# Reordering the first loads and the fillers, and holding back the second tile, at the head of a one-core FFT convolution

## The chip, the cores and the metric

The kernel runs on one core of one Trainium2 chip. The metric is the device time of an execution in microseconds (us). Within a time or a mean, a run is one execution; e1 to f4 below are experiments of several runs each. Where kernels are compared, they ran on the same chip in alternating rounds, and "ratio" is the mean time of one kernel's fast runs over the mean of the other's fast runs of the same rounds, so it is not quite the ratio of the medians that are quoted beside it. On one core a run is called slow when it is more than 1.5% above the fastest of its kernel. Lower is better, and a verdict of faster needs more than 2%.

## The reference

A 7 x 7 convolution of a 224 x 224 x 96 image, done through Fourier transforms, all in bf16 at the ends:

```python
x: (1, 224, 224, 96) bf16      w: (7, 7, 96, 96) bf16
wp = pad(w, to (224, 224))
Xf = rfft2(x over h, w);  Wf = rfft2(wp over h, w)
Yf = einsum('bhwi,hwio->bhwo', Xf, Wf)
y  = irfft2(Yf).astype(bf16)
```

## The kernel before

The kernel transforms along the image's height only, in blocks (matrix `Fm`), convolves along the width with few-tap products in that domain, and transforms back (matrix `G`). The image is cut into seven tiles of 32 columns. Each tile's pixels are loaded in two halves (`jg` 0 and 1, 118 rows each), multiplied by `Fm` on TensorE and evicted from PSUM into `xf`. The weights are loaded once as 98 rows and transformed by matmuls from `wq` into `WF`, in six groups; only the first group (48 matmuls, 12 evictions) is needed before the rounds can begin.

The head, all that comes before the first round, is what the change touches. First the loads, all issued by SyncE in this order: four small halo loads, the weights, the first tile, the second tile.

```python
for jg in range(2):
    load_rows(xh_bufs[jg], jg, W - PAD, PAD)                 # halo
dma(wqx[0:2*(PW-1), 0:C*C], bass.AP(wsrc.tensor, wsrc.offset, [[C*C, PW-1], [C2, 2], [1, C*C]]))   # 96 rows
for h in range(2):                                            # the last two rows, one by one
    n = C*C - h*C2
    dma(wqx[2*(PW-1)+h:2*PW-1+h, 0:n], wsrc[PW-1:PW, h*C2:])
for t in range(2):
    for jg in range(2):
        load_x(t, jg)                                         # 112 + 6 rows of 6,144 bytes each
...
warm(8); warm(9)                 # fillers: 128 x 512 matmuls on zeros, meant to keep TensorE's clock up
```

Then the order of work on TensorE, which follows the program:

```python
xf0 = new_xf(0)
for jg in range(2):
    for f in a_bank(0, xf0, xh_bufs[jg], 0, 3, jg, 0):        # halo: 12 matmuls
        f()
warm(8); warm(8)
fj = [f_jobs(0, p) for p in range(3)]
for f in prep_jobs(0) + fj[0][0] + fj[1][0] + fj[2][0] + fj[0][1]:
    f()                          # 48 weight matmuls, 96 on the first half of the pixels, 32 on the second
for f in jit(0, 0):              # sums on VectorE for the first rounds
    f()
...                              # rounds: products of xf and WF, each with more of the above as fill
```

## Time and profile before

How to read the lines: PE is TensorE (matmuls), PEld its weight loads, DVE is VectorE, ACT is ScalarE, POOL is GpSimd, and SP is SyncE, which issues the loads. A record is one instruction in the trace. The granted clock is the share of full speed at which TensorE is allowed to run (1.00 or 0.50 here). A frequency-domain matmul is one of `pb<-WF,xf`, the product of transformed weights and pixels; the first of them marks the end of the head.

| | before |
|---|---|
| median, and range of 4 runs | 295.09 us, 294.56 to 295.59 |
| span of the profiled run | 291.1 us (the run took 292.79 us, 2.3 us under the median) |
| TensorE idle before the weights | 6.00 us, from 10.45 to 16.44 us |
| TensorE idle at its 450th record | 2.28 us, from 24.23 to 26.51 us |
| half clock | 14.02 to 20.85 and 27.68 to 31.09 us, and the last 0.6 us |
| first frequency-domain matmul | 26.54 us |

The page's first line gives the busy time of each engine, its share of the span and the number of its instructions:

```profile
PE 268.3 (92%) x5227; PEld 242.7 (83%) x5227; DVE 223.2 (77%) x453; ACT 196.7 (68%) x485; POOL 113.8 (39%) x166
```

TensorE (PE) is the bound over the whole kernel, with 22.8 us of idle time in 291.1. Of these some 8.3 us are the two holes at the head. Busy time counts a matmul at half clock as longer (fillers follow one another every 0.23 us at full clock here, 16 in 3.62 us, and every 0.43 us at half clock in the changed kernel, from 21.09 us), so the half-clock stretches hide more of the loss inside the 268 us. How these places are found is told in the prediction.

### The profile page before, as it was taken

Reading aid. Unit: us, or ns where it says so; the run is one execution under the profiler, and the core shown is the slowest. Engines: PE = TensorE matmul, PEld = TensorE weight load, DVE = VectorE, ACT = ScalarE, POOL = GpSimd, SP = SyncE. Lnnn points to the kernel's source line nnn. Section 1 sums busy time; section 2 is a strip of 40 time slices with the busy share of each in tenths; the row PEclk is TensorE's granted clock in tenths of the full one; section 3 lists DMA queues with packets and bytes.
Section 4 is the critical chain, followed back from the end, with each engine's and each line's share of the span. In section 5 each row is a group of like instructions: output and inputs, shape, how many; then the busy total and the mean of one; then the engine's idle time right before and its main releaser. Section 6 shows DMA issues by size and latency. Waiting matters only on the chain.

```text
span 291.1 us, 12374 instructions
## 1 busy us (share of the span) xinstructions
PE 268.3 (92%) x5227; PEld 242.7 (83%) x5227; DVE 223.2 (77%) x453; ACT 196.7 (68%) x485; POOL 113.8 (39%) x166
## 2 busy tenths in 40 slices
PE   8476999899999979999999998999999999998982
PEld 4176999899999979988899987989898988886961
DVE  6146499888988869879977888787997789776823
ACT  6056997668764536886788867897788865657213
POOL 7711034248446564332643227222543324322100
PEclk9959899999999999999999999999999999999999
DMA  6993010441111289978659585787539543857846
GB/s 154 214 238 84 2 45 5 142 142 45 43 56 47 87 239 201 284 190 239 187 145 252 157 255 149 199 233 240 180 93 254 164 131 110 226 164 198 230 115 190
DMA packets 43857, 46.07 MB, mean 158 GB/s; under 512 B 33303, under 2 KB 34435, under 8 KB 43703
## 3 DMA queue, kind: packets, MB, share of 16 engines
q1 hardware_dynamic: 41512, 43.22, 53.9%
q10 hardware_dynamic: 2288, 2.06, 2.2%
q8 instruction: 41, 0.67, 1.0%
q14 instruction: 16, 0.12, 0.1%
HBM read 23.93 MB, written 21.33 MB: 155 GB/s over the span
## 4 chain that ended last, share of the span: by engine, by line
PE 59%; DVE 17%; DMA 11%; issue 4%; ACT 4%; POOL 1%; SPq 1%; DVEq 0%; ACTq 0%
PE pb L85 59%; DVE J L85 7%; DMA wq<-in_w_dram 4%; DVE WF L85 3%; DVE v L85 3%; DMA xn<-in_x_dram 2%; DVE u L85 2%; DVE yf L85 2%; DMA tt<-scr 1%; DMA out_dram<-yo 1%; DMA scrb<-yf 1%; ACT xf L85 1%; DMA xf<-scrb 1%; ACT WF L85 1%; SPq L85 1%
## 5 line engine op out<-in xcount | busy, mean ns | idle before, releaser
L85 PE MATMUL pb<-WF,J 96*128 96x96 bf16 x2898 | 169.0, 206 | 1.3 <-DVE u L85 0.8
L85 PEld LDWEIGHTS <-J 96*128 96x128 bf16 x2898 | 141.6, 98 | 17.0 <-issue 10.7
L85 POOL TENSOR_TENSOR yf<-v,u 128x384 bf16<-128x384 f32 x85 | 83.8, 1000 | 144.3 <-issue 96.4
L85 ACT CAST xf<-pb 96x408 bf16<-96x408 f32 (+3 forms) x146 | 68.6, 486 | 10.7 <-PE pb L85 8.3
L85 ACT CAST yo<-pb 84x384 bf16<-84x384 f32 (+1 forms) x144 | 61.4, 482 | 9.3 <-DMA out_dram<-yo 4.3
L85 DVE TENSOR_TENSOR J<-xf 96x1824 bf16<-96x1824 bf16 (+1 forms) x84 | 63.0, 789 | 0.1
L85 PE MATMUL pb<-WF,xf 96*128 96x96 bf16 x952 | 60.0, 206 | 0.1
L85 PEld LDWEIGHTS <-xf 96*128 96x128 bf16 x952 | 47.1, 98 | 2.6 <-issue 2.6
L85 PE MATMUL pb<-Fm,xn 118*128 118x136 bf16 (+3 forms) x640 | 46.0, 199 | 3.2 <-DMA xn<-in_x_dram 2.0
L85 PE MATMUL pb<-tt,Gm 102*84 102x384 bf16 (+1 forms) x144 | 36.3, 329 | 2.8 <-DVE u L85 1.2
L85 ACT CAST WF<-pb 96x480 bf16<-96x480 f32 (+1 forms) x63 | 31.2, 574 | 11.0 <-PE pb L85 10.9
L85 PEld LDWEIGHTS <-xn 118*128 118x128 bf16 x640 | 30.5, 97 | 3.6 <-DMA xn<-in_x_dram 2.2
L85 PE MATMUL pb<-wq 98*128 98x120 bf16 (+1 forms) x288 | 23.1, 240 | 6.0 <-DMA wq<-in_w_dram 6.0
L85 DVE TENSOR_TENSOR J<-J 96x912 bf16<-96x912 bf16 (+1 forms) x42 | 27.1, 646 | 0.0
L85 PEld LDWEIGHTS <-wq 98*128 98x128 bf16 x288 | 21.0, 151 | 6.5 <-issue 6.5
L85 POOL COPY xf<-xf 96x816 bf16<-96x816 bf16 (+3 forms) x20 | 17.3, 889 | 1.4 <-DVE xf L85 1.4
L85 DVE TENSOR_TENSOR yf<-v,u 128x384 bf16<-128x384 f32 x27 | 15.5, 575 | 0.9
L85 PE MATMUL pb<-wu 128*112 128x384 bf16 (+1 forms) x69 | 14.8, 375 | 1.1 <-DVE ct L85 1.1
L85 PEld LDWEIGHTS <-Gm 102*84 102x84 bf16 (+1 forms) x144 | 11.5, 114 | 4.0 <-issue 1.4
L85 PEld LDWEIGHTS <-wu 128*112 128x112 bf16 (+1 forms) x69 | 8.1, 119 | 6.7 <-issue 1.8
L85 DVE CAST WF<-pb 96x400 bf16<-96x400 f32 (+1 forms) x9 | 5.4, 604 | 9.4 <-PE pb L85 9.1
L85 DVE TENSOR_TENSOR WF<-WF 96x960 bf16<-96x960 bf16 x15 | 10.7, 763 | 0.6 <-ACT WF L85 0.6
(390 smaller groups left out, 219.8 us busy)
## 6 DMA issues: line engine op xcount, KB each, us to landing
scr<-yf SPq DMA_DIRECT2D x30, 288.0 KB
xn<-in_x_dram SPq DMA_DIRECT2D x12, 672.0 KB
tt<-scr SPq DMA_DIRECT2D x24, 288.0 KB
out_dram<-yo SPq DMA_DIRECT2D x24, 252.0 KB
tt<-scr SPq DMA_DIRECT2D x12, 192.0 KB
out_dram<-yo SPq DMA_DIRECT2D x12, 168.0 KB
wq<-in_w_dram SPq DMA_DIRECT2D x1, 1728.0 KB
WF<-in_x_dram SPq DMA_DIRECT2D x2, 672.0 KB
```

The source lines that it names most:

```text
L85: r = fn(*a, **k)
```

## The change

The intent: use the wait for the weights for half of the first tile's work, shorten the wait at its end, keep the second tile's 1.4 MB out of the way until the head is through, and place the fillers anew.

```diff
     for jg in range(2):
         load_rows(xh_bufs[jg], jg, W - PAD, PAD)
-    dma(wqx[0:2 * (PW - 1), 0:C * C], bass.AP(wsrc.tensor, wsrc.offset, [[C * C, PW - 1], [C2, 2], [1, C * C]]))
-    for h in range(2):
-        n = C * C - h * C2
-        dma(wqx[2 * (PW - 1) + h:2 * PW - 1 + h, 0:n], wsrc[PW - 1:PW, h * C2:])
-    for t in range(2):
-        for jg in range(2):
-            load_x(t, jg)
+    load_x(0, 0)
+    for k, n in ((0, PW - 1), (PW - 1, 1)):
+        dma(wqx[2 * k:2 * (k + n), 0:WC], bass.AP(wsrc.tensor, wsrc.offset + k * C * C, [[C * C, n], [C2, 2], [1, WC]]))
+    load_x(0, 1)
... (WC = C * C - C2; the matrix Em and the zeros behind it move to column WC; loads and evictions return their instruction)
-    warm(8)
-    warm(8)
     fj = [f_jobs(0, p) for p in range(3)]
-    for f in prep_jobs(0) + fj[0][0] + fj[1][0] + fj[2][0] + fj[0][1]:
+    for p in range(3):
+        for f in fj[p][0]:
+            f()
+    for _ in range(2):
+        warm(8)
+    for f in prep_jobs(0):
         f()
+    warm(4)
+    last = [f() for f in fj[0][1]]
+    for jg in range(2):
+        for d in load_x(1, jg):
+            tc.add_manual_dep(d.ins, last[0].ins.name, SYNC, reason="second tile's pixels later")
```

More of the change, by code (lines that the diff above doesn't have):

```diff
@@ L151 @@
     wq = wqx[0:PW2]
-    Em = wqx[0:PW2, C * C:C * C + 2 * NSLOT * NTAP].rearrange("p (h a t) -> p h a t", h=2, a=NSLOT)
+    WC = C * C - C2
+    Em = wqx[0:PW2, WC:WC + 2 * NSLOT * NTAP].rearrange("p (h a t) -> p h a t", h=2, a=NSLOT)
     XHW = PAD * C + 32
@@ L163, in ld @@
         def ld(p0, p1, hh):
-            dma(xb[p0:p1, 0:n], x[0, hh:hh + (p1 - p0), w0:w0 + npx, :].rearrange("h w c -> h (w c)"))
-        ld(PAD, R, h0 + PAD)
-        ld(0, PAD, h0 % H)
+            return dma(xb[p0:p1, 0:n], x[0, hh:hh + (p1 - p0), w0:w0 + npx, :].rearrange("h w c -> h (w c)"))
+        return ld(PAD, R, h0 + PAD), ld(0, PAD, h0 % H)
     def xbuf(t, jg):
@@ L171, in load_x @@
     def load_x(t, jg):
-        load_rows(xbuf(t, jg), jg, t * 2 * TW, 2 * TW)
+        return load_rows(xbuf(t, jg), jg, t * 2 * TW, 2 * TW)
     wsrc = w.rearrange("kh kw i o -> (kh kw) (i o)")
@@ L213 @@
     SE.activation(out=dmy[:], in_=pi_t[:], func=ACTF.Sin, bias=0.0, scale=0.0)
-    zw = wqx[0:PW2, C * C + 2 * NSLOT * NTAP:]
+    zw = wqx[0:PW2, WC + 2 * NSLOT * NTAP:]
     SE.copy(out=zw, in_=wu[0:PW2, 0:1].to_broadcast(list(zw.shape)))
@@ L432, in f @@
                 pi = pa[0:C, 0:(b - a) * n].rearrange("c (w r s j) -> c r s w j", r=2, s=s1 - s0, w=b - a)
-                apart(("A", t), (a, jg, ph, part), evac(xo, pi, (b - a) * n))
+                return apart(("A", t), (a, jg, ph, part), evac(xo, pi, (b - a) * n))
             return f
```

## The prediction

> **What bounds the kernel now.** I read the page first, then stretches cut at the steps of the granted clock, then the first 36 us of the chain of waits, the timeline there, and the records of packets and landings. The first two lines below are the page's busy digits and granted clock in 40 slices of 7.3 us.
>
> ```profile
> PE   8476999899999979999999998999999999998982
> ...
> PEclk9959899999999999999999999999999999999999
> ```
>
> From the sixth slice on TensorE is nearly full; the loss is in the first five slices, the head, and it is the only place besides the end where the clock falls. The stretches of 3.41 us show it (columns: stretch, length, busy us and count for PE, PEld, DVE, ACT and POOL, granted clock, DMA share, GB/s):
>
> ```profile
> 10.61:14.02 3.41, 0.00 (x0) 0.00 (x0) 0.00 (x0) 0.00 (x0) 2.77 (x11) 1.00 0.88 195
> 14.02:17.44 3.42, 1.00 (x13) 1.03 (x14) 0.11 (x1) 0.44 (x1) 1.81 (x5) 0.50 0.98 229
> 17.44:20.85 3.41, 3.41 (x47) 3.41 (x45) 2.69 (x5) 2.58 (x7) 0.00 (x0) 0.50 1.03 238
> 20.85:24.26 3.41, 3.38 (x123) 3.28 (x121) 3.17 (x7) 2.87 (x7) 0.00 (x0) 1.00 0.91 208
> 24.26:27.68 3.42, 1.17 (x22) 1.17 (x22) 1.09 (x3) 1.57 (x5) 1.00 (x3) 1.00 0.09 36
> 27.68:31.09 3.41, 3.41 (x51) 3.41 (x49) 2.67 (x4) 3.06 (x8) 0.30 (x1) 0.50 0.02 5
> ```
>
> Two holes stand out, at 10.45 to 16.44 us and at 24.23 to 26.51 us, and each is followed by a stretch at half clock. The timeline and the chain name what ended them:
>
> ```profile
> 16.44 3.77 PE L85 MATMUL pb<-wq 98*128 98x100 bf16 x43 [6.00 <-DMA wq<-in_w_dram]
> ...
> 26.51 0.19 PE L85 MATMUL pb<-Fm,WF 118*128 118x64 bf16 x1 [2.28 <-POOL xf L85]
> ```
> ```profile
> 3.61 12.70 DMA wq<-in_w_dram
> ```
>
> *First hole.* TensorE waits for the weights. The records of landings split the wait: the 96-row transfer is complete at 13.49 us, the first single row at 14.53, the second at 16.31. The packets of 18,432 bytes take 1.32 us in the median, and the two last rows follow one another (the last packet runs 13.11 to 14.89). So the last 2.82 us of the wait are two rows of 18 KB, queued behind each other.
>
> *Second hole.* It is put down to GpSimd's halo copy, which I don't believe: that copy ended at 26.10 and feeds the other buffer. What does fit is an instruction fetch. The trace has 41 packets of 16,384 bytes on the "instruction" queue for 10,516 TensorE records, 256 each. The first of them in the span runs from 23.80 to 25.06 us; TensorE stands still at its 450th record and goes on 1.45 us after the packet. The next packet starts at 27.91, 1.40 us after TensorE goes on. [...] The first-tile and second-tile pixels filled the DMA engines at that time (share 0.91 to 1.03), the second tile landing only at 27.12.
>
> [...] steps at 14.02, 20.85, 27.68 and 31.09 us, all multiples of 3.41 apart; a window only 1.17 us busy also led to half clock.
>
> **The change part by part.**
> 1. *First pixels ahead of the weights.* Two issues (0.3 to 0.4 us each) move in front of the weights; that alone costs nothing, because the rings are busy with the halo rows until 3.62 us. The data is what costs: 118 rows of 6,144 bytes, [...] a packet takes 0.415 us, so 8 x 0.415 = 3.3 us. Weight packets then start at about 6.9 instead of 3.88 us: +3.0 us.
> 2. *Last two rows in one transfer.* [...] So the weights should be complete at 14.53 + 3.0 = 17.5 us, against 16.31: they come 1.2 us later, where without this part it would be 3.0. All 18,336-byte rows are 0.5% shorter, which is nothing.
> 3. *Work moved into the hole.* The 96 matmuls on the first half (29 ns apart at full clock, 2.8 us) and their ten evictions (0.6 us each on two engines, 3 us) move from after the weights to about 7.5 to 10.5 us. Sixteen fillers (3.62 us before) then keep TensorE busy to about 14. Idle remains 14 to 17.5 us.
> 4. *After the weights.* 48 weight matmuls: 82 to 85 ns apart at half clock before, so 4.0 us; at full clock 62 ns (later weight matmuls), so 3.0 us. One window between 14 and 17.5 is mostly idle, so I count part of it at half clock: 3.6 us, to 21.2. Four fillers 0.9, to 22.1. Then 32 matmuls, 0.9, to 23.0. The second half of the pixels is ready: [...] weights through at 13.1 + 3.0 = 16.1, then 8 x 0.415, then up to 1 us of landing, so 20.4. The third of the last four evictions ends about 0.4 us after the last matmul: the first frequency-domain matmuls start at 23.4, against 26.54 before: **-3.1 us**.
> 5. *Instruction block.* [...] the 2.28 us stall goes. This is contained in point 4, not added to it.
> 6. *Clock after the head.* Without the second hole there should be no half-clock stretch from 27.68 to 31.09. It held 51 matmuls; at full clock that is about 1.7 us less TensorE time, but ACT was 3.06 us busy in the same stretch, and the chain goes over to ACT's weight evictions at 30.75. I count half: **-0.8 us**.
> 7. *Second tile held.* Issued near 22.3 us, landed after about 1.2 us of issue and start and 3.1 us for each half: 26.6 and 29.7. In the kernel before, the first half was used 8.3 us and the second 12.2 us after the first frequency-domain matmul, so at 31 and 35 here: hidden. Its 1.4 MB do meet the next instruction block[...]: 0 to 1 us, counted as 0.
>
> Sum: 3.1 + 0.8 = 3.9 us. From 60 to 280 us TensorE is 97% busy in an unchanged program, so a shift of the head should reach the end whole. 294.73 - 3.9 = 290.8.
>
> **The rivals.**
> *The weights' delay eats the gain.* If TensorE falls to half clock for everything from 17.5 on, fillers included (0.43 us each, as the first six fillers show), the last matmul of the head is at 17.5 + 4.0 + 1.7 + 1.8 = 25.0, a gain of 1.5 us only: 293.2. For it: idle of 3.5 us, [...]
> *The stall moves.* The held pixels occupy the engines just when the next block is fetched; [...] up to 1 us back, 291.8. For it: the delay seen before. [...]
> *Everything goes well.* If the landing's lag of 1.4 us shrinks and the clock holds, the first frequency-domain matmul is at 21.5 to 22, and the half-clock stretch is all gain: 5.5 to 6 us, 289. For it: the fillers were surely sized for it. Against: the bytes ahead of the weights can't be argued away.
> *The gain is lost in 30 to 50 us.* There ACT and DVE are on the chain, evicting weights and first products. Those jobs are unchanged and start earlier with the head; I see nothing absolute in time there except the second tile's arrival, with 4 us to spare.
>
> **Range and chances.** The two bad rivals together make about 293, the good one 289; nothing brings it over 295 unless the held pixels arrive late. 2% is 5.9 us and needs every uncertain term on the good side: 14%. Slower by 2% would need a new wait of 10 us: 2%.
>
> **What would show it.** Weights complete at 17 to 18 us and the 96 early matmuls before 11; no hole of 2 us near the 450th TensorE record; the first frequency-domain matmul between 22 and 24.5; granted clock full from about 24 us; second tile's pixels landed before they are read. It would be wrong if the weights land after 18.5 us, if TensorE stops again for an instruction block at 27 to 30 us, or if the second tile is waited for near 31 us.

## The result

The changed kernel took 291.41 us in the median (290.87 to 292.21, 4 runs) against 295.09 us (294.56 to 295.59, 4 runs): 3.7 us less. The ratio is 0.9878, with a 95% interval of 0.9846 to 0.991: by the 2% rule the same, yet clear of noise. The prediction had 290.8 us, 3.9 us under the 294.73 us that it started from. Two later measurements of the same kernel on other chips gave 0.9846 and 0.9869.

The profile after, first the page's busy line and its rows of 40 slices:

```profile
PE 271.0 (94%) x5231; PEld 243.1 (84%) x5231; DVE 223.9 (77%) x453; ACT 197.2 (68%) x485; POOL 114.9 (40%) x166
...
PE   8959998999999979999999998999999999999982
...
PEclk9988999799999999999999999999999999999998
```

The second slice of TensorE, 4 before, is 9, and the third, now with the rest of the wait for the weights, is 5 instead of 7; the clock now also dips in the eighth slice, near 51 us, where it was full before. Next the stretches between the steps of the clock (columns as in the prediction):

```profile
16.69:20.10 3.41, 2.25 (x36) 2.28 (x37) 1.77 (x4) 1.52 (x4) 0.00 (x0) 1.00 0.25 69
20.10:23.52 3.42, 3.42 (x33) 2.32 (x32) 1.42 (x3) 1.38 (x4) 0.00 (x0) 0.50 0.00 0
23.52:26.93 3.41, 2.97 (x74) 2.85 (x72) 3.03 (x5) 3.07 (x8) 1.98 (x3) 1.00 0.58 156
26.93:30.34 3.41, 3.41 (x79) 3.41 (x76) 1.28 (x2) 3.41 (x10) 0.33 (x1) 1.00 0.95 267
```

The half-clock stretch at 27.68 us is gone: 79 matmuls run in 3.41 us where 51 did. But one of 3.41 us lies within the head, from 20.10 us, and only 33 matmuls start in it. The timeline shows which (columns: start, length, engine, operation, count; in brackets the idle time before and what ended it):

```profile
8.61 2.69 PE L85 MATMUL pb<-Fm,WF 118*128 118x64 bf16 x96 [0.35 <-DMA WF<-in_x_dram]
...
11.15 3.61 PE L85 MATMUL pb<-wu 128*128 128x512 bf16 x16
...
17.85 3.44 PE L85 MATMUL pb<-wq 98*128 98x100 bf16 x48 [3.09 <-DMA wq<-in_w_dram]
...
21.09 1.91 PE L85 MATMUL pb<-wu 128*128 128x512 bf16 x4
...
22.79 1.44 PE L85 MATMUL pb<-Fm,WF 118*128 118x64 bf16 x32
...
24.66 0.52 PE L85 MATMUL pb<-WF,xf 96*128 96x96 bf16 x8 [0.44 <-ACT xf L85]
```

The 96 early matmuls fill part of the wait. The weights come at 17.72 us, the 48 weight matmuls still run mostly at full clock, and then the four late fillers take 1.91 us at half clock, before the last 32 matmuls. The first frequency-domain matmul (`WF,xf`) starts at 24.66 us, 1.9 us earlier than before. The hole of 2.28 us is gone.

Between these two profiles the spans differ by only 2.0 us (289.1 against 291.1), less than the 3.7 us between the medians. Two things make the difference. The profile of before was of a run 2.3 us under its median, that of after of a run 0.5 us under. And the clock dip near 51 us cost the changed kernel a part of its gain. The stretches there, changed kernel first:

```profile
47.41:50.82 3.41, 2.30 (x62) 2.19 (x60) 3.41 (x8) 2.91 (x7) 2.12 (x3) 1.00 0.02 5
50.82:54.24 3.42, 3.42 (x56) 3.42 (x53) 1.69 (x4) 1.36 (x3) 1.15 (x2) 0.50 0.69 214
```

Then the same place in a later profile of the same changed kernel (run f1 below):

```profile
47.29:50.70 3.41, 2.33 (x66) 2.21 (x65) 3.41 (x9) 2.32 (x6) 1.67 (x3) 1.00 0.00 0
50.70:54.11 3.41, 3.41 (x82) 3.41 (x79) 2.46 (x5) 2.12 (x6) 1.02 (x1) 1.00 0.92 270
```

Both have the same hole of 1.1 us in the first stretch (TensorE waits there for VectorE), once followed by half clock and once not. The busy time of a stretch of 3.41 us alone does not settle it in these profiles: stretches with 2.25 us (16.69 to 20.10 us) and 2.30 us of TensorE work were followed by half clock, the one with 2.33 us (f1) was not, and in the first profile after, one with 1.5 us (13.27 to 16.69 us) was not either. What settles it is not shown. From the 33rd to the 101st frequency-domain matmul the program took 19.4 us with the dip and 18.1 us without: 1.3 us that have nothing to do with what was changed. The third profile's span is 286.6 us, 2.5 us under the first of the very same kernel. So one profile of each kernel doesn't size this change; the milestones of the head, and the timed runs, do.

### The profile page after: what moved, and what is told of

Its sections match the earlier page's. It is cut to its first block, busy times and chain, and to the rows that moved or that the text cites. A ratio compares the mean times of both kernels' runs of the same rounds, so it can differ in the third digit from the quotient of the medians.

```text
span 289.1 us, 12381 instructions
## 1 busy us (share of the span) xinstructions
PE 271.0 (94%) x5231; PEld 243.1 (84%) x5231; DVE 223.9 (77%) x453; ACT 197.2 (68%) x485; POOL 114.9 (40%) x166
## 4 chain that ended last, share of the span: by engine, by line
PE 60%; DVE 17%; DMA 10%; ACT 5%; issue 4%; SPq 1%; POOL 1%; ACTq 0%; DVEq 0%
PE pb L85 60%; DVE J L85 7%; DMA wq<-in_w_dram 5%; DVE WF L85 3%; DVE v L85 3%; DVE u L85 2%; DMA xn<-in_x_dram 2%; ACT WF L85 2%; DVE yf L85 2%; ACT xf L85 1%; DMA xf<-scrb 1%; DMA tt<-scr 1%; DMA scrb<-yf 1%; SPq L85 1%; ACT yo L85 1%
## 5 line engine op out<-in xcount | busy, mean ns | idle before, releaser
L85 PEld LDWEIGHTS <-J 96*128 96x128 bf16 x2898 | 141.7, 98 | 15.7 <-issue 9.3
L85 ACT CAST xf<-pb 96x408 bf16<-96x408 f32 (+2 forms) x147 | 69.2, 487 | 14.1 <-PE pb L85 11.9
L85 PE MATMUL pb<-wq 98*128 98x120 bf16 (+1 forms) x288 | 22.1, 232 | 3.1 <-DMA wq<-in_w_dram 3.1
L85 PEld LDWEIGHTS <-wq 98*128 98x128 bf16 x288 | 20.1, 151 | 3.6 <-issue 3.6
L85 PE MATMUL pb<-wu 128*128 128x512 bf16 (+1 forms) x73 | 18.0, 410 | 1.1 <-DVE ct L85 1.1
L85 POOL COPY xf<-xf 96x816 bf16<-96x816 bf16 (+3 forms) x20 | 18.3, 944 | 0.0
L85 PEld LDWEIGHTS <-wu 128*128 128x128 bf16 (+1 forms) x73 | 8.9, 125 | 8.2 <-issue 4.1
```

The source lines that it names most:

```text
L85: r = fn(*a, **k)
```

## The experiments

Twelve experiments went to three chips, four on each. All gave correct outputs. In the table "ratio" is against the kernel before in the same rounds, "first" is the start of the first frequency-domain matmul in the run's profile, and "half clock" is the mean time at half clock in the fast runs, worked out as 2 x (1 - granted clock) x span from the clock that each run lists (it holds up to 4 us at the end of the profiled runs, where TensorE has no work). By the 2% rule each of these ratios is "same" or "unclear"; an interval that stays below 1 is clear of noise all the same.

| run | what | ratio (95% interval) | first, us | mean us of fast runs | half clock, us |
|---|---|---|---|---|---|
| before, chip A | | | 26.54 (first profile) | 294.32 | 14.6 |
| e1 | changed, again | 0.9846 (0.9788 to 0.9903) | 24.92 | 289.78 | 8.5 |
| e2 | changed, second tile not held | 0.9876 (0.9823 to 0.993) | 24.78 | 290.68 | 8.5 |
| e3 | changed, last rows apart | 0.9852 (0.9799 to 0.9904) | 24.77 | 289.95 | 6.7 |
| e4 | changed, fillers early only | 0.9784 (0.9733 to 0.9836) | 21.76 | 287.98 | 3.6 |
| before, chip B | | | | 292.25 | 10.0 |
| e5 | before + hold | 0.9954 (0.9928 to 0.998) | 24.93 | 291.45 | 9.2 |
| e6 | before, many small fillers | 1.0028 (1.0004 to 1.0052) | 27.36 | 292.68 | 14.1 |
| e7 | before + hold + two rows in one | 0.9907 (0.9875 to 0.9938) | 23.58 | 290.38 | 7.6 |
| e8 | changed, no fillers | 0.9975 (0.9949 to 1.0) | 22.69 | 292.40 | 15.7 |
| before, chip C | | | | 293.85 | 12.9 |
| f1 | changed, third time | 0.9869 (0.9796 to 0.9941) | 23.95 | 289.92 | 8.8 |
| f2 | fillers early only, again | 0.9824 (0.9749 to 0.99) | 22.57 | 288.94 | 6.3 |
| f3 | no fillers, again | 0.996 (0.993 to 0.999) | 22.82 | 292.69 | 15.3 |
| f4 | before's order + hold + two rows + fillers early | 0.9838 (0.9761 to 0.9914) | 22.99 | 289.02 | 4.4 |

A caution on chip B: the kernel before ran 75 times there, from 289.24 to 300.66 us, and the fast 289.24 puts 27 runs above the 1.5% line, so its mean of fast runs is cut low. Over all runs the four ratios of that chip would be 0.9950, 0.9990, 0.9926 and 0.9979; the order of the four is the same. On chip C 9 of the 27 runs of before are left out in the same way; over all runs the ratios there would be 0.9834, 0.9801, 0.9928 and 0.9804. So a ratio depends on this cut by up to 0.4%.

### e1: the changed kernel again

No edit.

> The changed kernel, unedited, for a tighter interval and to see whether the halved clock falls at the same places. My theory: 0.987 to 0.989 of the kernel before. [...]

The median was 290.17 us against 294.12 (ratio 0.9846, a little better than expected). The clock was half from 16.50 to 23.32 and from 50.63 to 54.04 us, where the first profile had 20.10 to 23.52 and 50.82 to 54.24. So the stretch in the head moved and became twice as long; the one near 51 us was in the same place to within 0.2 us. Yet e2, e3 and f1, which run the same program there, have none at 51 us. So the place in the program alone is not enough for it; what else it takes is not shown.

### e2: the second tile not held

```diff
     load_x(0, 1)
+    for jg in range(2):
+        load_x(1, jg)
...
-    for jg in range(2):
-        for d in load_x(1, jg):
-            tc.add_manual_dep(d.ins, last[0].ins.name, SYNC, ...)
```

> The changed kernel with the second tile's pixels issued straight after the first tile's, as before. My theory: [...] no hole over 0.5 us near the 450th TensorE record, time within 0.5 us of the changed kernel (ratio to before 0.986 to 0.990). Rival: holding the pixels is what freed the engines for the block; then a hole of 1 to 2.3 us comes back near the 450th or 700th record and the time is 292.5 to 293.5 us (0.992 to 0.996).

No hole came back near the 450th record or the 700th: the largest before 45 us, after the weights, is the 0.46 us wait for the last eviction. The median was 290.90 us and the ratio 0.9876, within the expected range, and not to be told from e1. The timeline has the weights 0.8 us later, at 18.4 us, and the first frequency-domain matmul where e1 has it:

```profile
18.53 3.99 PE L85 MATMUL pb<-wq 98*128 98x100 bf16 x48 [3.86 <-DMA wq<-in_w_dram]
...
24.78 0.51 PE L85 MATMUL pb<-WF,xf 96*128 96x96 bf16 x8 [0.46 <-ACT xf L85]
```

In the changed order, then, the hold is worth nothing that these runs can show; with six runs of each, 2 us in the mean would be needed.

### e3: the last two weight rows apart

```diff
-    for k, n in ((0, PW - 1), (PW - 1, 1)):
-        dma(wqx[2*k:2*(k+n), 0:WC], ...)
+    dma(wqx[0:2*(PW-1), 0:WC], ...)
+    for h in range(2):
+        dma(wqx[2*(PW-1)+h:2*PW-1+h, 0:WC], wsrc[PW-1:PW, h*C2:h*C2+WC])
```

> The changed kernel with the last two weight rows again as two transfers of one row. My theory: [...] the weights are complete 1.5 to 2 us later (about 19.4 us), and the time rises by about as much: 292.8 to 293.3 us, ratio 0.992 to 0.995. Rival: the second half of the first pixels sets the end of the head (19.44 us) and hides it; then the time is as that of the changed kernel within 0.5 us.

The expectation fell. By the records of landings the first of the two rows was complete at 16.62 us and the second at 18.28: 1.7 us apart, as expected. But with both rows in one transfer the wait for the weights had ended at 17.6 us in e1, not at 16.6, so the separate second row cost 0.7 us and not 1.5 to 2. Even that is not clear: with both rows in one transfer and the second tile held, the last row landed anywhere from 16.9 to 17.9 us in seven profiles of this order. And it did not reach the rounds:

```profile
18.33 3.94 PE L85 MATMUL pb<-wq 98*128 98x100 bf16 x48 [4.52 <-DMA wq<-in_w_dram]
22.07 1.31 PE L85 MATMUL pb<-wu 128*128 128x512 bf16 x4
24.77 0.52 PE L85 MATMUL pb<-WF,xf 96*128 96x96 bf16 x8 [0.46 <-ACT xf L85]
```

The clock came back to full at 22.64 us, within the late fillers, which took 1.31 us (1.83 in e1, where it came back at 23.32 us); so the 0.7 us were made up there. The rival in the expectation (the second half of the pixels hides it) named the right outcome with a wrong cause: those pixels had landed before the fillers began.

### e4 and f2: fillers early only

```diff
-    for _ in range(2):
-        warm(8)
+    for n in (8, 8, 7, 6):
+        warm(n)
     for f in prep_jobs(0):
         f()
-    warm(4)
```

> The changed kernel with 13 more fillers before the weights (to fill 14.8 to 17.7 us) and none after the weight matmuls. My theory: the clock stays full from 6 us on, the weight matmuls are through at 20.9 us, the four late fillers (1.91 us in the profile of the changed kernel) go, and the first frequency-domain matmuls start at 22.5 to 23 instead of 24.66 us: 1.5 to 2 us less, 289.4 to 290 us, ratio 0.980 to 0.984. Rival: evictions of the weight matmuls or the second half of the pixels set the pace of that stretch, or the fillers run past the arrival of the weights: no gain, 0.986 to 0.990.

> The kernel with 13 more fillers before the weights and none after, again (its first profile fell in a slow execution). My theory: the gain of the head of 2.9 us reaches the end as soon as no slow transfer or halved clock near 105 us takes it: 0.977 to 0.983, below the changed kernel by 0.5% to 1%; no halved clock before 45 us. Rival: a wait near 105 us for the third tile's pixels is fixed in time and takes the gain back: equal to the changed kernel within 0.3%.

The head did as expected in both: no half clock before 100 us, the weight matmuls at full clock, no fillers behind them. This is f2:

```profile
10.71 6.42 PE L85 MATMUL pb<-wu 128*128 128x512 bf16 x29
18.06 3.12 PE L85 MATMUL pb<-wq 98*128 98x100 bf16 x48 [0.93 <-DMA wq<-in_w_dram]
21.02 1.10 PE L85 MATMUL pb<-Fm,WF 118*128 118x64 bf16 x32
22.57 0.52 PE L85 MATMUL pb<-WF,xf 96*128 96x96 bf16 x8 [0.46 <-ACT xf L85]
```

The medians were 288.16 us (ratio 0.9784) and 288.81 us (0.9824), beside 0.9846 and 0.9869 for the changed kernel on the same chips. It is the better of the two on both chips, by 0.6% and 0.45%; the intervals overlap, so the order is likely rather than proven. Against the kernel before the gain is clear of noise. The head gained more than that, 1.4 to 3.2 us. Part went at a later wait, for the third tile's pixels. First f2's, then f1's, the changed kernel on the same chip:

```profile
103.94 0.34 PE L85 MATMUL pb<-Fm,xn 118*128 118x136 bf16 x3 [3.09 <-DMA xn<-in_x_dram]
```
```profile
103.36 0.34 PE L85 MATMUL pb<-Fm,xn 118*128 118x136 bf16 x3 [1.13 <-DMA xn<-in_x_dram]
```

f2 arrived 1.4 us earlier at this wait and left it 0.6 us later. In f2 and in e4's slow-state profile the wait was 3 us or more; in the other profiles of all kernels it was 1.1 to 2.4 us. Half clock followed in f2 and e4, and also in e5, e7 and f3, whose waits were 2.2 to 2.4 us. The profiled run of f2 was also the slowest of its six (290.51 us), that of f1 the second fastest of its six (288.33 us). Two profiles are too few to say that an earlier arrival lengthens it, so whether the rival (a wait fixed in time) holds in part stays open.

### e5: the kernel before with the hold alone

```diff
-    for t in range(2):
-        for jg in range(2):
-            load_x(t, jg)
+    for jg in range(2):
+        load_x(0, jg)
...
-    for f in prep_jobs(0) + fj[0][0] + fj[1][0] + fj[2][0] + fj[0][1]:
+    for f in prep_jobs(0) + fj[0][0] + fj[1][0] + fj[2][0]:
         f()
+    last = [f() for f in fj[0][1]]
+    (the hold, as in the change)
```

> The kernel before with one thing changed: the second tile's pixels are held until the first eviction of the last head group. The weights still come at 16.3 us. My theory (the hole at the 450th TensorE record is an instruction block delayed by pixel traffic): the block's packet starts at about 22 instead of 23.80 us, the hole of 2.28 us shrinks to 0 to 0.6 us and the first frequency-domain matmul comes at 24.7 to 25.2 instead of 26.54 us; ratio 0.990 to 0.995. Rival (the hole is a wait for GpSimd's copy, as the profile names it): the hole stays at 2.3 us and the time within 0.3% of before.

The hole is gone, and the packet of the instruction block, at 23.80 us before, starts at 19.80 us, sooner than I had expected. That is 0.3 us before the 194th record runs (20.10 us), which lies one packet's worth of records, 256, before the 450th; so it is not the run of that record that asks for the block:

```profile
16.19 4.19 PE L85 MATMUL pb<-wq 98*128 98x100 bf16 x48 [5.74 <-DMA wq<-in_w_dram]
20.18 3.99 PE L85 MATMUL pb<-Fm,WF 118*128 118x64 bf16 x128
24.93 0.51 PE L85 MATMUL pb<-WF,xf 96*128 96x96 bf16 x8 [0.76 <-ACT xf L85]
```

All 128 pixel matmuls run in one piece, where the last had stood still for 2.28 us, and the next ones wait 0.76 us for their eviction. GpSimd's instructions were not touched, so the profile's releaser was wrong. The median is 291.20 us against 293.08, the ratio 0.9954, just outside the range expected: 1.6 us at the head, and less of it in the timed mean.

### e6: the kernel before with many small fillers

```diff
-    warm(8)
-    warm(8)
+    for _ in range(2):
+        pwu = bank()
+        for _ in range(32):
+            TE.matmul(pwu[:, 0:128], lhsT=wu[:, 0:128], rhs=wu[:, 0:128], start=True, stop=True)
```

> The kernel before with its sixteen fillers of 512 columns replaced by 64 of 128 columns: about the same TensorE time before the weights, but 96 more instruction records, no transfer moved. My theory: [...] no hole over 0.5 us at the 450th record nor at the place of the old one, first frequency-domain matmul at 24.7 to 25.5 us, ratio 0.990 to 0.995. Rivals: a wait for GpSimd's copy would keep the hole at the same matmul; an instruction block delayed by traffic whenever asked for would move it to the 450th record, 96 records earlier in the program, with a hole of 1 us or more.

My theory failed here and its second rival was right:

```profile
20.28 2.99 PE L85 MATMUL pb<-Fm,WF 118*128 118x64 bf16 x80
24.83 2.29 PE L85 MATMUL pb<-Fm,WF 118*128 118x32 bf16 x48 [1.56 <-issue]
27.36 0.82 PE L85 MATMUL pb<-WF,xf 96*128 96x96 bf16 x8 [0.25 <-ACT xf L85]
```

The hole is again at the 450th record, which is now the 81st pixel matmul instead of the 128th. No wait of the program was moved there; the profile itself has only "issue" as its releaser. That settles what the hole is: a matter of counted instructions. But coming to the 194th record sooner did not help. It came at 16.3 us instead of 20.4, and the packet still started only at 22.20 us, in the midst of the pixel traffic (the pixels' queue filled 84.7% of the engines' time from 22.15 to 23.5 us). Nor was it ahead of the wait for the weights: records 191 and 192 are TensorE's own waits, the second of them ending with the weights at 16.2 us, so the 194th came just behind the wait. Half clock for 6.8 us followed, and the kernel was no better than before (median 292.77 us, ratio 1.0028).

What the profiles show of the packet is its start: 23.80 us (before) and 22.20 us (e6) with the second tile's pixels on their way, 19.80 us without them (e5). That it waits behind them is my guess from these three; no run shows it. In the changed kernel the 194th record came at 10.4 us and the packet ran from 15.98 to 17.54 us, beginning beside the last weight packet (14.70 to 16.30 us); TensorE reached its 450th record at 23.9 us and did not stop there.

### e7: the kernel before with the hold and the two rows in one transfer

The edits of e5, and the weights' two transfers as in the change.

> The kernel before with the hold and with the last two weight rows in one transfer: everything in the change but the pixels ahead of the weights, the new order and the new fillers. My theory: weights complete at 14.5 to 14.9 us, weight matmuls at half clock to 18.8, pixels there at about 18 and 21, first frequency-domain matmul at 23 to 24 us, against 24.66 in the changed kernel: ratio 0.985 to 0.990, as good as the whole change. Rival: putting half the pixels ahead is what pays; then this gains no more than the hold alone, 0.991 or more.

```profile
14.95 3.43 PE L85 MATMUL pb<-wq 98*128 98x100 bf16 x48 [2.93 <-DMA wq<-in_w_dram]
18.18 4.63 PE L85 MATMUL pb<-Fm,WF 118*128 118x64 bf16 x128
23.58 0.52 PE L85 MATMUL pb<-WF,xf 96*128 96x96 bf16 x8 [0.76 <-ACT xf L85]
```

In this order the two rows do pay: the weights come 1.2 us earlier than in e5 and the rounds begin 1.35 us earlier. At 23.58 us the first frequency-domain matmul lies before that of the changed kernel in any of its three profiles. The ratio, 0.9907 (0.9875 to 0.9938), is between the two theories' ranges: 0.5% better than the hold alone (the intervals overlap slightly), and just behind the changed kernel's 0.9846 to 0.9878, measured on other chips.

### e8 and f3: the changed kernel without the fillers

```diff
-    for _ in range(2):
-        warm(8)
     for f in prep_jobs(0):
         f()
-    warm(4)
```

> The changed kernel without the sixteen fillers ahead of the weights and without the four after them. My theory: TensorE is idle from 11.1 to 17.7 us, so the weight matmuls run at half clock (4.0 instead of 3.2 us) and the last 32 at 1.1 to 2 us, but the 1.9 us of the late fillers go: first frequency-domain matmul at 24 to 24.7 us, so the fillers as they stand bring nothing: within 0.3% of the changed kernel, 0.985 to 0.990. Rival: fillers are what makes the change pay; then it comes at 25.5 us or later and the ratio is 0.991 or more.

> The changed kernel without any new or old fillers before the weights or after, again: its profile showed the first frequency-domain matmul 2 us earlier than the changed kernel, yet its times were only 0.25% under before. Theory: [...] the clock is half for 3.4 or 6.8 us and often into the rounds after the head; then this profile shows another place of the half clock and a later first frequency-domain matmul, 23.5 to 25 us, and a ratio above that of the changed kernel by 0.5% or more. Rival: the times of the earlier runs were those of that chip; then it is equal to the changed kernel here within 0.3%.

Both profiles show a better head than the changed kernel's; this is f3:

```profile
17.30 4.12 PE L85 MATMUL pb<-wq 98*128 98x100 bf16 x48 [6.79 <-DMA wq<-in_w_dram]
22.82 0.51 PE L85 MATMUL pb<-WF,xf 96*128 96x96 bf16 x8 [0.46 <-ACT xf L85]
```

The weight matmuls run at half clock, and the four late fillers are missing: 22.8 us, earlier than 24 to 24.7 expected. Yet the ratios, 0.9975 and 0.996, are those of e8's rival (0.991 or more) and not "within 0.3% of the changed kernel", and the times were the worst of all variants of the change, 292.74 and 292.76 us in the median of 22 runs each, on two chips. My theory for f3, that another run would show the first frequency-domain matmul late, fell: f3 has the half clock from 14.4 us again and the same start; only its ratio came as that theory said, and its rival (equal to the changed kernel) fell too.

What the times do show is the clock: 15.7 and 15.3 us at half clock in the mean, against 8.5 and 8.8 us for the changed kernel. f3's profile has 6.8 us of it in the head, 3.4 us at 48.5 and 3.4 us at 106.5 us. The difference of means on chip C, 292.69 - 289.92 = 2.8 us for 15.3 - 8.8 = 6.5 us more at half clock, is 0.43 us for each us. Within single kernels, a line through all runs of one gives 0.23 to 0.47 us for each us in the sets of 22 to 75 runs (0.14 to 0.38 through the fast runs alone). So more half clock goes with a longer time by roughly this size; that it is the cause of these 2.8 us is argued and not shown. In f3's profile 1.5 us are lost from the 33rd to the 101st frequency-domain matmul, about 2 us from the 201st to the 401st (a wait of 2.19 us for pixels near 104, then half clock), and another 2 us from the 601st to the last, each against f1. Why a kernel without fillers at the head meets more half clock later is not shown by these runs, and stays open; one profile per run gives the place of half clock in one run only.

### f1: the changed kernel, third time

No edit.

> The changed kernel once more, beside the next three on one chip, because the four runs before had no changed kernel of their own beside them. My theory: 0.985 to 0.989; a halved clock somewhere between 16 and 24 us, from the idle time of 3 us ahead of the weights.

The median is 290.56 us against 294.97, the ratio 0.9869; the first frequency-domain matmul is at 23.95 us, and the clock is half from 18.3 to 21.7 us, in the range foreseen, and nowhere else before the end.

### f4: the order of before, with hold, two rows and early fillers

The kernel of e7, with `warm(8); warm(8)` made `for n in (8, 8, 7, 6): warm(n)`.

> The order of before (weights ahead of all pixels) with the hold, the two rows in one transfer, and 13 more fillers so that TensorE is busy until the weights come at about 14.9 us. My theory: full clock all through the head, weight matmuls to 18.1, then 128 matmuls whose 14 evictions (0.3 us apart) and the landing of the second half at about 20.5 set the pace: first frequency-domain matmul at 22 to 22.8 us, ratio 0.980 to 0.986, so putting pixels ahead of the weights is worth at most 1 us. Rival: the early half is what counts; then 23.5 us or later and 0.989 or more.

```profile
15.59 3.12 PE L85 MATMUL pb<-wq 98*128 98x100 bf16 x48 [1.26 <-DMA wq<-in_w_dram]
18.60 3.63 PE L85 MATMUL pb<-Fm,WF 118*128 118x64 bf16 x128
22.99 0.51 PE L85 MATMUL pb<-WF,xf 96*128 96x96 bf16 x8 [0.76 <-ACT xf L85]
```

The clock was full until the end of the work, at 282.5 us. The first frequency-domain matmul came 0.2 us later than I had expected, and the ratio is 0.9838 as expected. Its mean, 289.02 us, is that of f2 (288.94) on the same chip. So with the fillers set right, putting half of the pixels ahead of the weights brings nothing that these runs can show: the three plain edits to the kernel before do the same, to within 2 us (six runs of each). In the profiles f2 and e4 reach the first frequency-domain matmul 0.4 and 1.2 us sooner than f4.

## Why the prediction was right, point by point

The total was right: 3.9 us foreseen, 3.7 us in the medians, and 291.41 us lies between its good case (289) and its bad ones (about 293). Its parts fared differently.

1. *First pixels ahead of the weights*: right in kind, mis-sized. They were to delay the weights by 3.0 us, my estimate from eight packets of 0.415 us in a row; that eight follow one another is not shown, and the 118 packets of the first half took 0.28 us in the median in the profile after. The first weight packet started at 5.90 us instead of the 6.9 foreseen, 2.0 us later than before (3.88), and in e3, with the rows apart as before, the last row landed at 18.28 us against 16.31: again 2.0 us. The 96 early matmuls ended at 11.3 us in the first profile, slightly later than the 11 foreseen.
2. *Last two rows in one transfer*: mis-sized too. In the first profile of the changed kernel the two rows were complete at 16.84 and 17.72 us, 0.88 us apart, where before they were complete 1.78 us apart (14.53 and 16.31). I put its worth in the changed order at 1.8 us (1.2 instead of 3.0 us of delay). e3 shows 0.7 us at the weights and nothing at the rounds. *The weights at 17.5 us* came true (17.72, 17.6 and 17.45 us in three profiles of the changed kernel) because a cost 1 us too large and a saving 1.1 us too large cancel, and that is luck. In the order of before it is worth 1.2 us at the weights (e5 to e7), where nothing behind it takes it up.
3. *Work moved into the hole*: right as to the work, and idle from 14.8 to 17.7 us against 14 to 17.5 foreseen.
4. *After the weights, -3.1 us*: this is the term whose mis-sizing shows in the time. It measured -1.9, -1.6 and -2.6 us (24.66, 24.92 and 23.95 against 26.54). The first two starts lie outside the 22 to 24.5 us that the prediction named as its sign. The clock fell as foreseen, but it was half until 23.5, 23.3 and 21.7 us, so that the late fillers took 1.91, 1.83 and 1.24 us instead of 0.9; and the last 32 matmuls took 1.44, 1.10 and 1.10 us instead of 0.9. After work resumed, half clock went on for 4.4 us in the profile before (16.44 to 20.85 us) and for 5.6 us in e1 (17.72 to 23.32). e4 and f2 show this directly: without those fillers and with full clock the start is at 21.76 and 22.57 us.
5. *Instruction block*: right that the hole is one (e5, e6) and that it goes. How it goes is shown only in part. In e6 TensorE came to its 194th record 4 us earlier than before and had the hole all the same. In the changed kernel it came there at 10.4 us, the packet ran from 15.98 to 17.54 us, and the 450th record followed at 23.9 us, 6.4 us after the packet's end. When a block is asked for, and what it waits for, is not shown.
6. *Clock after the head, -0.8 us*: the half-clock stretch went. From the first to the 33rd frequency-domain matmul the program took 16.80 us before and 16.37, 16.36 and 16.40 us after: 0.4 us, half of what I counted. But I looked only at this one stretch. In the timed runs the change spends 8.5 and 8.8 us at half clock against 14.6 and 12.9 us of before on the same chips, 4 to 6 us less. With 0.3 us for each us, the slope in all runs of before, that is an estimated 1.2 to 1.8 us; with the 0.2 of the fast runs alone it is 0.8 to 1.2 us. Part of it lies within the head and is in the gain there already.
7. *Second tile held*: right. The second tile landed at 29.1 and 31.7 us; its first half was first read at 31.64 us. No new hole came from the next instruction block, whose packet started at 24.02 us, ahead of most of the pixels.

So at the 33rd frequency-domain matmul the gain is 2.3, 2.1 and 3.0 us (43.34 us before; 41.03, 41.28 and 40.35 after), less than the 3.9 us of the sum; the rest of the timed gain goes with less half clock in general, which is argued from those slopes and not shown. That the total came out although point 4 was too large and point 6 looked at one stretch only is luck too. Of the rivals, the first (half clock eats the gain) took about 1 us of it, the second (the stall moves) did not occur, and the third (everything goes well) is what e4 is.

The hold and the rows are cures for trouble of the order of before. In that order they are worth 1.6 and 1.35 us at the head; once half of the pixels go ahead, taking either of them out costs nothing that shows. Taking out both together, and the new order alone in the kernel before, were not tried.

## What to carry to other kernels

When a change bundles several cures, try each alone and each left out: here two that were worth 3 us together in one order were worth nothing that shows in the other, and three small edits matched the whole. A filler paid here when it filled a wait that was there anyway up to its end, and cost when it stood between arrived data and their use (0.9784 and 0.9824 with early fillers alone, 0.9846 and 0.9869 with four of them behind the weights, which took 1.2 to 1.9 us there). And if an engine with small instructions stops at a place where nothing was waited for, count its instructions: here TensorE stopped at its 450th record in two kernels (before and e6), and the packet of 16,384 bytes on the instruction queue started 4 us later with 1.4 MB more of pixels on their way (23.80 us against 19.80 in e5).
